# Attention, Fourier mixing and feed-forward on one core: packed constants, cross-wise folds, special columns as two column groups, a new order

## The chip, the cores and the metric

The kernel runs on one core of one Trainium2 chip. A time is the device time of one execution in microseconds (us); what is compared is the median over several executions. A profile is one execution recorded by the hardware: its span runs from the first to the last instruction, and the time of that execution is a little longer than its span.

The engines are TensorE (PE, whose weight loads are listed as PEld), VectorE (DVE), ScalarE (ACT), GpSimd (POOL) and SyncE (SP, which only issues DMAs here). Each works through its own instructions in program order and waits on semaphores for the others.

## The reference

Three stages follow each other for 8 batches, 576 positions and 8 heads of 64 (512 columns).

```python
# attention: local band plus a pooled copy (positions averaged by 4)
q_d, k_d, v_d = (t.reshape(B, H, S // 4, 4, D).mean(3) for t in (q, k, v))
out_up = np.repeat(softmax_attention(q_d, k_d, v_d), 4, axis=2)
out_local = softmax_attention(q, k, v, mask=abs(i - j) < 4)
x = (out_up + out_local) -> [8, 576, 512]
# mixing
mixed = real(fft(fft(x, axis=1), axis=2))
u = x + mixed
# feed-forward, 512 -> 2048 -> 512
un = (u - mean(u)) / sqrt(var(u) + 1e-6)
out = u + relu(un @ w_ch1) @ w_ch2
```

## The kernel before

**Attention.** A `Unit` is a span of 128 positions of one batch (5 per batch, 40 in all). Its steps are `load` (queries and keys, 512 KB), `load_v`, `sum_in` (sums over 4 positions, DVE, line 697), `scores` (PE: four matmuls that put the band mask into the banks, line 707, and then 16 of queries with keys, line 714), `maxima` (DVE, line 726), `exps` (ACT), `transpose_p` (PE, with the identity as an operand, line 746), `copy_p`, `values` and `result`, which leaves the rows of the front half of a batch in `xa` and those of the back half, mirrored, in `xb`. `Pooled` does the same for the averaged sequence of a batch, once all five `sum_in` are done; its first PE step is line 567, and it leaves its rows in `odt`.

**Mixing.** The transform of a real sequence is done by folding. `Mix.half_sum` (DVE, line 838) and `half_difference` (POOL, line 841) make `xa + xb` and `xa - xb`. `channels` (DVE, line 849) adds to, or takes from, each its own mirror over the columns, `fold` (DVE and POOL, line 862) halves the columns once more, `sequence` (PE, line 887) multiplies by cosines and sines over positions, and `mix` (PE) by those over columns. Columns 0 and 256 have no mirror: `split_z` copies them to `zs`, `sequence_z` (PE, line 902) takes 4 matmuls with 66 columns of weights each, which add up in one bank, and `z_high` and `z_low` store the 4 rows of the result in two parts in `yz`, which `clear_yz` has set to zero.

**Feed-forward.** Rows are taken in nine blocks of 512. `Quarter` decodes the weights, which are given as 64-bit floats: `fetch` (SP), `size` (ACT), `clamp` (POOL), `join` (three DVE instructions, lines 448, 451 and 454), `high` (ACT) and `low` (POOL), 64 times. `Block.first` (line 1266) and `Block.second` (lines 1286 to 1288) are the two products, and `Block.finish` (DVE, line 1292) empties a bank of the second into the output rows. Blocks 0 and 1 start with the first five of 16 weight chunks and go on when more are decoded; blocks 3 and up use a scheme with fewer products (line 1204).

**Order.** Each call of `at` takes its place from the table `TURNS`, one row of numbers for each step; all steps are issued in the order of these places, on every engine, and PSUM banks are handed out in that order. Steps from block 3 on have times worked out by formula in place of table entries.

**Start.** SP issues the identity `ident` first, then the loads. POOL issues two DMAs that convert to 16 bits on the way, `identb` (line 480) and `maskb` (line 482); both are operands of the band mask's matmuls. Meanwhile PE runs 40 matmuls of 128 columns on zeros (`WARM_UP`, line 1400).

Of the kernel before, what the change touches and what calls it, by code (L numbers as in the profile page):

```python
# [22 lines left out]
ZCOLS = 66  # L23
# [4 lines left out]
        55, 125, 253, 392, 518, 667, 797, 918,  # L28
    ),
    "Pooled.copy_v": (  # L30
        59, 129, 262, 399, 521, 670, 806, 926,
    ),
    "Pooled.scores": (
        41, 22, 34, 150, 78, 115, 263, 204, 230, 411, 346, 361, 523, 483, 501, 671, 627, 646, 803, 755, 764,
        934, 866, 899,
    ),
    "Pooled.maxima": (
        43, 26, 39, 152, 85, 118, 271, 212, 232, 417, 352, 379, 529, 490, 516, 680, 632, 647, 820, 757, 770,
        940, 873, 904,
    ),  # L40
    "Pooled.exps": (
        54, 32, 40, 165, 101, 121, 272, 220, 248, 424, 353, 384, 533, 498, 520, 686, 634, 665, 821, 762, 782,
        944, 875, 919,
    ),
    "Pooled.transpose_p": (
        65, 38, 42, 188, 104, 136, 303, 233, 268, 436, 369, 414, 557, 509, 526, 711, 644, 682, 840, 767, 810,
        951, 881, 931,
    ),
    "Pooled.copy_p": (
        70, 47, 64, 200, 120, 148, 308, 240, 270, 437, 382, 423, 563, 519, 541, 712, 662, 687, 847, 775, 818,  # L50
        953, 886, 941,
    ),
    "Pooled.values": (
        72, 62, 66, 211, 145, 151, 316, 275, 285, 446, 403, 432, 576, 527, 551, 720, 675, 717, 856, 809, 845,
        967, 927, 947,
    ),
    "Pooled.result": (
        79, 63, 71, 217, 147, 161, 322, 277, 297, 456, 405, 448, 580, 536, 556, 721, 679, 719, 869, 811, 857,
        970, 935, 956,
    ),  # L60
    "Pooled.store": (
        109, 187, 404, 453, 653, 768, 868, 973,
    ),
    "Pooled.pack": (
        95, 229, 332, 489, 606, 734, 891, 976,
    ),
    "Mix.half_sum": (
        108, 134, 127, 258, 237, 254, 360, 395, 373, 515, 506, 517, 642, 639, 643, 751, 788, 774, 907, 913,
        932, 993, 980, 996,
    ),  # L70
    "Mix.half_difference": (
        111, 97, 113, 241, 216, 225, 356, 368, 370, 508, 485, 547, 626, 684, 683, 793, 829, 795, 900, 905,
        912, 1005, 978, 994,
    ),
    "Mix.channels": (
# [4 lines left out]
    ),  # L80
    "Mix.fold": (
# [4 lines left out]
    ),  # L86
    "Mix.split_z": (
        133, 157, 189, 267, 380, 421, 468, 558, 637, 700, 787, 815, 922, 939, 1002, 1006,
    ),
    "Mix.sequence_z": (  # L90
        185, 290, 458, 559, 714, 824, 986, 1015,
    ),
    "Mix.z_high": (
        207, 304, 469, 573, 715, 835, 991, 1053,
    ),
    "Mix.z_low": (
        214, 311, 486, 578, 725, 843, 1013, 1083,
    ),
    "Mix.sequence": (
        202, 191, 169, 170, 323, 337, 336, 330, 487, 479, 452, 450, 619, 610, 585, 590, 752, 743, 735, 727,  # L100
        848, 854, 878, 887, 1001, 997, 1000, 990, 1040, 1059, 1071, 1076,
    ),
    "Mix.sequence_out": (
        206, 180, 350, 342, 495, 462, 624, 591, 760, 758, 860, 892, 1012, 1017, 1073, 1105,
    ),
    "Mix.mix": (
        231, 246, 228, 239, 354, 374, 378, 398, 355, 408, 497, 512, 507, 582, 631, 655, 641, 673, 678, 696,
        778, 781, 765, 769, 911, 979, 921, 954, 903, 897, 1085, 1093, 1034, 1084, 1112, 1219, 1203, 1291,
        1143, 1152,
    ),  # L110
# [4 lines left out]
    "Mix.unfold": (
        255, 257, 243, 251, 385, 381, 400, 416, 442, 427, 524, 538, 604, 594, 664, 661, 676, 692, 708, 707,
        807, 805, 779, 791, 1044, 1045, 1033, 1007, 920, 917, 1145, 1134, 1096, 1110, 1250, 1259, 1297, 1303,
        1177, 1184,
    ),
    "Mix.store_mixed": (  # L120
        298, 438, 616, 716, 901, 1064, 1238, 1307,
    ),
    "Mix.store_local": (
        112, 117, 287, 261, 389, 406, 534, 542, 691, 702, 756, 837, 906, 957, 989, 998,
    ),
    "Mix.store_ends": (
        543, 858, 1042, 1286,
    ),
    "Unit.load": (
        0, 4, 13, 1, 8, 50, 52, 14, 35, 48, 76, 182, 141, 91, 143, 252, 307, 222, 329, 249, 375, 434, 209,  # L130
        413, 415, 513, 588, 548, 572, 540, 697, 600, 672, 690, 654, 789, 784, 825, 763, 801,
    ),
    "Unit.sum_in": (
        3, 9, 16, 6, 12, 58, 68, 51, 44, 57, 168, 192, 197, 183, 198, 341, 345, 328, 339, 276, 463, 476, 473,
        477, 449, 611, 605, 613, 599, 587, 747, 674, 693, 713, 738, 808, 846, 862, 827, 859,
    ),
# [12 lines left out]
    "Unit.exps": (
        11, 15, 36, 73, 56, 89, 114, 124, 155, 173, 226, 238, 282, 260, 325, 288, 394, 409, 454, 467, 504,  # L150
        562, 570, 584, 586, 615, 629, 677, 706, 744, 740, 802, 814, 832, 852, 896, 908, 960, 950, 972,
    ),
    "Unit.transpose_p": (
        19, 25, 53, 77, 90, 99, 132, 159, 160, 205, 250, 245, 305, 289, 331, 410, 401, 422, 455, 472, 528,
        568, 583, 593, 607, 622, 636, 699, 718, 745, 772, 816, 828, 870, 867, 910, 930, 964, 958, 982,
    ),
    "Unit.copy_p": (
        21, 29, 69, 80, 102, 106, 137, 172, 171, 213, 269, 256, 317, 300, 338, 419, 418, 426, 465, 474, 554,
        575, 595, 602, 617, 649, 638, 709, 728, 753, 785, 836, 851, 871, 880, 914, 936, 969, 968, 983,
    ),  # L160
    "Unit.values": (
        28, 67, 86, 87, 107, 164, 146, 190, 178, 218, 295, 306, 321, 333, 348, 431, 420, 464, 471, 496, 560,
        603, 612, 620, 633, 736, 701, 726, 766, 759, 823, 853, 872, 885, 888, 938, 955, 981, 971, 987,
    ),
# [3 lines left out]
    ),  # L168
    "constants": (
        135,  # L170
    ),
    "clear_yz": (
        176,
    ),
# [1372 lines left out]
```

## Time and profile before

| | |
|---|---|
| median of 3 runs | 1107.03 us (1103.9 to 1108.41) |
| time of the profiled execution | 1109.62 us |
| its span | 1107.6 us |
| busy in the span: PE, DVE, ACT, POOL | 1064.3, 635.5, 401.4, 349.3 us |
| mean granted clock of PE | 0.994 |
| HBM read and written | 166.86 MB, 45.42 MB |

The busy time of an engine is an average over stages with different limits, so the rows below are by stage. A busy PE is one with a matmul in flight; how many matmuls share the array can't be seen from it, only from the distances between starts. In a row of a timeline a group's length is that of its last end, and the next group may start before it.

### The profile page before, as it was taken

What the parts mean: (1) busy time and instruction counts of PE and PEld (TensorE: products, weight loads), DVE (VectorE), ACT (ScalarE), POOL (GpSimd) and SP (SyncE); (2) the same over time, 40 slices, a digit from 0 to 9 for tenths busy, and PEclk for the clock granted to TensorE, in tenths of its full rate; (3) what the DMA queues carried; (4) which work ended last, traced back from release to release, by engine and by line L of the source; (5) the groups of instructions that cost most, each with busy time, mean ns of one, the idle gap of its engine ahead of it and who ended that gap; (6) DMA issues with size and microseconds to landing.
All of it is one profiled execution on the core that took longest, in us unless ns stands there. A gap on an engine that the chain in (4) does not pass through costs nothing.

```text
span 1107.6 us, 24297 instructions
## 1 busy us (share of the span) xinstructions
PE 1064.3 (96%) x9316; PEld 892.8 (81%) x9316; DVE 635.5 (57%) x1298; ACT 401.4 (36%) x1122; POOL 349.3 (32%) x501
## 2 busy tenths in 40 slices
PE   6899999999989999999999999999999999999998
PEld 5676676777768788888788898899988889988997
DVE  5888989898797884442423533534443443353333
ACT  5765676655434442221312321231231232232121
POOL 1323223234554545655612131140230331221000
PEclk8999999999999999999999999999999999999999
DMA  7767668763845555748619546955954964975641
GB/s 269 227 199 236 198 227 250 226 182 115 228 99 170 156 156 185 168 140 223 185 65 283 192 155 197 300 160 176 318 177 141 294 210 150 243 252 180 218 153 38
DMA packets 121451, 214.36 MB, mean 194 GB/s; under 512 B 14576, under 2 KB 30992, under 8 KB 121208
## 3 DMA queue, kind: packets, MB, share of 16 engines
q1 hardware_dynamic: 110056, 191.97, 52.7%
q0 software_dynamic: 11280, 20.84, 10.6%
q8 instruction: 74, 1.21, 0.4%
q14 instruction: 41, 0.34, 0.1%
HBM read 166.86 MB, written 45.42 MB: 192 GB/s over the span
## 4 chain that ended last, share of the span: by engine, by line
PE 71%; DMA 12%; DVE 9%; issue 3%; ACT 2%; SPq 1%; POOL 1%; DVEq 0%; ACTq 0%; POOLq 0%
PE banks L1204 19%; PE banks L1286 10%; PE banks L1287 10%; PE banks L1288 10%; PE banks L1266 8%; PE banks L887 3%; DMA w1l<-ut 3%; DMA qkT<-in_qk_dram 3%; DMA raw<-in_wq_dram 2%; PE banks L926 2%; PE banks L616 1%; DMA w1h<-ut 1%; PE banks L1133 1%; PE banks L774 1%; PE banks L746 1%
## 5 line engine op out<-in xcount | busy, mean ns | idle before, releaser
L1286 PE MATMUL banks<-w2h,hh 128*128 128x512 f32 x576 | 228.0, 396 | 0.0
L1287 PE MATMUL banks<-w2l,hh 128*128 128x512 f32 x576 | 225.4, 391 | 0.0
L1288 PE MATMUL banks<-w2h,hl 128*128 128x512 f32 x576 | 224.9, 390 | 0.2 <-DVE hl L1274 0.2
L1270 ACT ACTIVATE hh<-row 128x512 fp32r<-128x512 f32 x96 | 60.6, 632 | 282.9 <-DVE row L1229 188.2
L1229 DVE TENSOR_TENSOR row<-wt,banks 128x256 f32<-128x256 f32 x192 | 80.3, 418 | 141.9 <-PE banks L1204 137.5
L1274 DVE SCALAR_TENSOR_TENSOR hl<-row,hh 128x512 fp32r<-128x512 f32 x96 | 68.9, 718 | 119.6 <-ACT hh L1270 119.6
L1288 PEld LDWEIGHTS banks<-w2h,hl 128*128 128x128 f32 x576 | 108.2, 188 | 24.3 <-DVE hl L1274 0.6
L1286 PEld LDWEIGHTS banks<-w2h,hh 128*128 128x128 f32 x576 | 108.5, 188 | 19.8
L1287 PEld LDWEIGHTS banks<-w2l,hh 128*128 128x128 f32 x576 | 108.6, 188 | 19.3
L1266 PE MATMUL banks<-unT,w1h 128*128 128x512 f32 x384 | 103.7, 395 | 3.5 <-DVE ut L1292 2.2
L1266 PEld LDWEIGHTS banks<-unT,w1h 128*128 128x128 f32 x384 | 72.4, 189 | 20.1 <-DVE ut L1292 2.7
L1103 POOL DMA_DIRECT2D ut<-ux x40 | 34.8, 941 | 162.4 <-DMA ut<-um 133.1
L1274 DVE SCALAR_TENSOR_TENSOR hl<-banks,hh 128x512 fp32r<-128x512 f32 x48 | 32.6, 686 | 74.6 <-ACT hh L1270 74.5
L1224 ACT COPY wt<-banks 128x256 f32<-128x256 f32 x96 | 35.7, 372 | 97.2 <-PE banks L1204 97.0
L733 ACT ACTIVATE sb<-banks,mx 128x64 f32<-128x64 f32 x320 | 69.8, 329 | 1.4 <-PE banks L746 0.2
L887 PE MATMUL banks<-seq,f 128*128 128x290 f32 x256 | 67.8, 414 | 0.9 <-issue 0.6
L1204 PE MATMUL banks<-w1h,w1h 128*128 128x256 f32 x384 | 62.0, 283 | 2.6 <-DMA w1h<-ut 1.5
L1204 PE MATMUL banks<-w1h,w1l 128*128 128x256 f32 x384 | 62.5, 285 | 2.0 <-DMA w1l<-ut 1.5
L1270 ACT ACTIVATE hh<-banks 128x512 fp32r<-128x512 f32 x48 | 28.5, 597 | 98.5 <-PE banks L1287 62.4
L1204 PE MATMUL banks<-unT,w1h 128*128 128x256 f32 x432 | 63.3, 283 | 0.7 <-DVE row L1229 0.7
L1204 PEld LDWEIGHTS banks<-unT,w1h 128*128 128x128 f32 x432 | 59.8, 191 | 4.7 <-DVE row L1229 0.9
L1204 PE MATMUL banks<-unT,w1l 128*128 128x256 f32 x432 | 63.2, 282 | 0.0
(122 smaller groups left out, 1944.0 us busy)
## 6 DMA issues: line engine op xcount, KB each, us to landing
w1l<-ut SPq DMA_DIRECT2D x96, 256.0 KB
w1h<-ut SPq DMA_DIRECT2D x96, 256.0 KB
qkT<-in_qk_dram SPq DMA_DIRECT2D x40, 512.0 KB
w1h<-ub SPq DMA_DIRECT2D x72, 256.0 KB
w1l<-ub SPq DMA_DIRECT2D x72, 256.0 KB
raw<-in_wq_dram SPq DMA_DIRECT2D x64, 256.0 KB
vaug<-in_vw_dram SPq DMA_DIRECT2D x40, 260.0 KB
out_dram<-ut SPq DMA_DIRECT2D x36, 256.0 KB
```

Of the source, the lines that this page charges most:

```text
L733: nc.scalar.activation(out=self.sb[:, hp, z], in_=self.sc[:, z, hp], func=AF.Exp, scale=0.125, bias=self.mx[:, z, hp : hp + 1],)
L887: nc.tensor.matmul(y, l, r, start=(i == 0), stop=(i == len(mms) - 1))
L1103: nc.gpsimd.dma_start(out=to, in_=ux[b][k0 : k0 + m, :], accum_op=ALU.add)
L1204: nc.tensor.matmul(into, w[:, y, c, :], both[z][:, c, :], start=(start and i == 0), stop=(i == len(mms) - 1), skip_group_check=True)
L1224: nc.scalar.copy(out=joins[k].bitcast(F32), in_=self.ps[x])
L1229: nc.vector.tensor_add(out=place(to), in0=place(a), in1=self.ps[x])
L1266: nc.tensor.matmul(hps, a[:, c, :], unT[:, x, c, :], start=(i == 0), stop=(i == len(mms) - 1))
L1270: nc.scalar.activation(out=hh, in_=self.hps[f], func=AF.Relu)
L1274: nc.vector.scalar_tensor_tensor(out=hl, in0=self.hps[f], scalar=0.0, in1=self.hh[f].bitcast(F32), op0=ALU.max, op1=ALU.subtract)
L1286: nc.tensor.matmul(acc, hh, w2h, start=start, stop=False)
L1287: nc.tensor.matmul(acc, hh, w2l, start=False, stop=False)
L1288: nc.tensor.matmul(acc, hl, w2h, start=False, stop=stop)
```

## The change

**Constants at the start.** Identity and mask arrive as 16-bit numbers that the host has packed in pairs into 32-bit words, in one tile `bits` (48 KB), by SP's first DMA. The full identity moves from SP's queue to POOL's, as the first DMA there. `WARM_UP` goes from 40 to 28.

**Cross-wise folds.** `half_sum` and `half_difference` become `cross`: `p` is `xa` plus the column mirror of `xb` (DVE), `q` is `xb` plus the column mirror of `xa` (POOL), 255 columns each where the former two took 512. `channels` then takes `p + q` and `p - q`, so each of its instructions reads what both engines made.

**Special columns.** `zs` has 32 columns a slot where it had 66. Of the four matmuls of `sequence_z` two write rows 0 to 31 and two write rows 32 to 63 of the bank. `z_high` and `z_low` store all 64 rows of each part, so `clear_yz` goes, and `signs` sums the two groups in `mix`. `split_z` adds the columns from `xa` and `xb` on POOL, where ACT had copied them.

**Order.** Every entry of `TURNS` is new up to the start of the fourth block.

```diff
-WARM_UP = 40
+WARM_UP = 28
...
-    nc.sync.dma_start(out=ident, in_=c_ident)
+    nc.gpsimd.dma_start(out=ident, in_=c_ident)
...
-    identb = pd.tile([P, P], BF16, name="identb", bufs=1)
-    nc.gpsimd.dma_start(out=identb, in_=c_ident)
-    maskb = pd.tile([P, W], BF16, name="maskb", bufs=1)
-    nc.gpsimd.dma_start(out=maskb, in_=c_mask)
+    bits = pd.tile([P, P + W], BF16, name="bits", bufs=1)
+    nc.sync.dma_start(out=bits.bitcast(F32), in_=c_bits)
+    identb, maskb = bits[:, :P], bits[:, P:]
...
-        def half_sum(self, t):
-            nc.vector.tensor_add(out=halves[0][:, t, :DM], in0=xa[:, t], in1=xb[:, t])
-
-        def half_difference(self, t):
-            nc.gpsimd.tensor_sub(out=halves[1][:, t, :DM], in0=xa[:, t], in1=xb[:, t])
+        def cross(self, t, back):
+            near, far = (xb, xa) if back else (xa, xb)
+            (nc.gpsimd if back else nc.vector).tensor_tensor(
+                out=crossed[back][:, t, 1:HD], in0=near[:, t, 1:HD], in1=far[:, t, DM - 1 : HD : -1], op=ALU.add
+            )
...
-            src = odt[:, 0] if t == NSL else halves[odd][:, t]
+            if t == NSL:
+                a, b = odt[:, 0, 1:HD], odt[:, 0, DM - 1 : HD : -1]
+            else:
+                a, b = (x[:, t, 1:HD] for x in crossed)
...
-            nc.scalar.copy(out=z[:, :, 0:2], in_=x)
+                nc.scalar.copy(out=zs[:, NSL:, 0:2], in_=odt[:, 0:1, cols])
             else:
+                nc.gpsimd.tensor_add(out=zs[:, :NSL, 0:2], in0=xa[:, :, cols], in1=xb[:, :, cols])
...
-            y = self.yzp = bank(self, "yz", ZCOLS)[:, 0, :KEPT]
-            mms = self.slots(zs, 0)
-            for i, (l, r) in enumerate(mms):
-                nc.tensor.matmul(y, l, r, start=(i == 0), stop=(i == len(mms) - 1))
+            y = self.yzp = bank(self, "yz", 2 * ZCOLS)[:, 0, :KEPT]
+            for i, (l, r) in enumerate(self.slots(zs, 0)):
+                g = i % 2 * ZCOLS
+                nc.tensor.matmul(y[g : g + ZCOLS], l, r, start=(i < 2), stop=(i >= 2), skip_group_check=True)
```

The order shows at three places. On DVE, the first sums (697 before, 690 after the change), maxima (726, 719) and pooled maxima (572, 565) at the program's start, before:

```order
L697 TENSOR_REDUCE sums<-qkT 128x8x32
L726 TENSOR_REDUCE mx<-banks 128x8
L697 TENSOR_REDUCE sums<-qkT 128x8x32 x2
L726 TENSOR_REDUCE mx<-banks 128x8
L697 TENSOR_REDUCE sums<-qkT 128x8x32
L697 TENSOR_REDUCE sums<-qkT 128x8x15
L697 TENSOR_REDUCE sums<-qkT 128x8x17
L726 TENSOR_REDUCE mx<-banks 128x8
L572 TENSOR_REDUCE mxd<-banks 128x4
```

and of the change:

```order
L690 TENSOR_REDUCE sums<-qkT 128x8x32
L719 TENSOR_REDUCE mx<-banks 128x8
L690 TENSOR_REDUCE sums<-qkT 128x8x32
L719 TENSOR_REDUCE mx<-banks 128x8
L690 TENSOR_REDUCE sums<-qkT 128x8x32
L719 TENSOR_REDUCE mx<-banks 128x8
L690 TENSOR_REDUCE sums<-qkT 128x8x15
L690 TENSOR_REDUCE sums<-qkT 128x8x17
L719 TENSOR_REDUCE mx<-banks 128x8
L690 TENSOR_REDUCE sums<-qkT 128x8x32
L565 TENSOR_REDUCE mxd<-banks 128x4
```

Sums and maxima now take turns, and four units have their maxima ahead of the fifth unit's sum, where two had.

On PE, around the second batch's `sequence_z`, before:

```order
L714 MATMUL banks<-qkT 64x64 x16
L616 MATMUL banks<-vsum,ptd 64x65 x16
L746 MATMUL banks<-ident,sb 128x128 x4
L902 MATMUL banks<-seq,z 66x290 x4
L774 MATMUL banks<-vaug,pT 64x65 x16
```

and of the change:

```order
L700 MATMUL banks<-bits 64x256
L707 MATMUL banks<-qkT 64x64 x16
L891 MATMUL banks<-seq,z 32x290 x4
L609 MATMUL banks<-vsum,ptd 64x65 x16
L767 MATMUL banks<-vaug,pT 64x65 x16
```

The four matmuls, now of 32 columns of weights, stand between the scores of a unit and the pooled values, where a transpose had stood ahead of them.

On DVE, where block 1's first five weight chunks are done and its banks are emptied (line 1292 before, 1282 after the change) between joins of decoded weights (448, 451 and 454; 442, 445 and 448), before:

```order
L1292 TENSOR_TENSOR ut_4797<-banks,ut_4797 128x512
L1292 TENSOR_TENSOR ut_4798<-banks,ut_4798 128x512
L448 TENSOR_SCALAR wt<-wt 128x256
L451 SCALAR_TENSOR_TENSOR wt<-raw,wt 128x256
L454 SCALAR_TENSOR_TENSOR wt<-raw,wt 128x256
L448 TENSOR_SCALAR wt<-wt 128x256
L451 SCALAR_TENSOR_TENSOR wt<-raw,wt 128x256
L454 SCALAR_TENSOR_TENSOR wt<-raw,wt 128x256
L1292 TENSOR_TENSOR ut_4800<-banks,ut_4800 128x512
```

and of the change:

```order
L1282 TENSOR_TENSOR ut_4785<-banks,ut_4785 128x512
L442 TENSOR_SCALAR wt<-wt 128x256
L445 SCALAR_TENSOR_TENSOR wt<-raw,wt 128x256
L448 SCALAR_TENSOR_TENSOR wt<-raw,wt 128x256
L1282 TENSOR_TENSOR ut_4787<-banks,ut_4787 128x512
L1282 TENSOR_TENSOR ut_4788<-banks,ut_4788 128x512
```

Three banks are emptied with one join between them, where two joins stood ahead of the third.

## Rows read from the trace of the kernel before

**Rows 1.** Busy time by stage: us, PE, PEld, DVE, ACT, POOL, clock, DMA, GB/s.
```profile
0.00:20.00 20.00, 12.49 (x240) 10.76 (x240) 9.53 (x15) 7.74 (x28) 3.65 (x15) 0.83 0.92 342
20.00:60.00 40.00, 33.01 (x783) 23.93 (x787) 35.22 (x76) 30.99 (x115) 9.52 (x15) 0.96 0.63 210
60.00:280.00 220.00, 211.25 (x3779) 155.54 (x3770) 197.94 (x421) 138.99 (x486) 71.07 (x97) 1.00 0.66 203
280.00:400.00 120.00, 113.73 (x496) 90.66 (x495) 99.78 (x199) 49.42 (x121) 64.97 (x105) 0.99 0.56 160
400.00:1108.00 708.00, 693.78 (x4037) 611.89 (x4035) 293.00 (x590) 174.30 (x375) 200.08 (x270) 1.00 0.63 191
```

**Rows 2.** PE timeline, 0 to 14 us: start, length, work, idle before and releaser.
```profile
1.01 4.45 PE L1400 MATMUL banks<-raw 128*128 128x128 bf16 x40 [1.01 <-DVE raw L1397]
8.54 0.30 PE L707 MATMUL banks<-maskb,identb 64*64 64x256 bf16 x4 [3.08 <-DMA maskb<-in_c_mask_dram]
8.65 0.90 PE L714 MATMUL banks<-qkT 64*64 64x64 f32 x32
```

**Rows 3.** DVE timeline, 0 to 15 us.
```profile
5.00 1.22 DVE L697 TENSOR_REDUCE sums<-qkT 128x256 f32<-128x1024 f32 x1 [4.04 <-DMA qkT<-in_qk_dram]
9.64 0.69 DVE L726 TENSOR_REDUCE mx<-banks 128x8 f32<-128x512 f32 x1 [3.43 <-PE banks L714]
10.25 2.33 DVE L697 TENSOR_REDUCE sums<-qkT 128x256 f32<-128x1024 f32 x2
```

**Rows 4.** PE timeline, 12.5 to 16.5 us.
```profile
15.55 1.23 PE L567 MATMUL banks<-sums 64*64 64x160 f32 x16 [2.45 <-DVE sums L697]
```

**Rows 5.** DMA issues: last figure is median us from issue to landing.
```profile
identb<-in_c_ident_dram POOLq DMA_DIRECT2D x1, 32.0 KB, 5.1
```

**Rows 6.** POOL timeline, 0 to 4 us.
```profile
1.25 0.74 POOL L480 DMA_DIRECT2D identb<-in_c_ident_dram  x1 [0.82 <-POOLq L1530]
```

**Rows 7.** PE timeline, 85.9 to 89 us.
```profile
86.27 2.12 PE L902 MATMUL banks<-seq,z 128*66 128x290 f32 x8
88.32 0.70 PE L774 MATMUL banks<-vaug,pT 64*64 64x65 f32 x32
```

**Rows 8.** PE timeline, 181.9 to 184.2 us.
```profile
182.35 1.69 PE L541 MATMUL banks<-vaug,poolm 128*32 128x260 f32 x20
183.97 0.50 PE L567 MATMUL banks<-sums 64*32 64x160 f32 x16
```

**Rows 9.** DVE groups by shape, 0 to 290 us: busy us, mean ns.
```profile
L838 DVE TENSOR_TENSOR xs<-xa,xb 128x512 f32<-128x512 f32 x24 | 19.1, 800 | 0.3 <-DVE f L862 0.3
...
L849 DVE TENSOR_TENSOR w<-xm 128x255 f32<-128x255 f32 x24 | 12.8, 542 | 0.1
...
L849 DVE TENSOR_TENSOR w<-xs 128x255 f32<-128x255 f32 x24 | 10.5, 437 | 0.0
```

**Rows 10.** POOL groups by shape, 0 to 300 us.
```profile
L841 POOL TENSOR_TENSOR xm<-xa,xb 128x512 f32<-128x512 f32 x24 | 32.5, 1368 | 34.4 <-DVE xb L794 21.1 <-DMA xa<-rest 6.6 <-DVE rs L791 5.2
L862 POOL TENSOR_TENSOR f<-w 128x256 f32<-128x256 f32 x32 | 26.7, 839 | 43.7 <-DVE w L849 30.5 <-DVE rs L791 12.8 <-DVE rsd L628 0.4
```

**Rows 11.** PE timeline, 365 to 380 us.
```profile
365.83 1.07 PE L1266 MATMUL banks<-unT,w1h 128*128 128x512 f32 x4
...
368.55 0.39 PE L1286 MATMUL banks<-w2h,hh 128*128 128x512 f32 x1
...
373.67 1.71 PE L1266 MATMUL banks<-unT,w1h 128*128 128x512 f32 x4 [2.24 <-DVE ut L1292]
...
378.12 0.40 PE L1286 MATMUL banks<-w2h,hh 128*128 128x512 f32 x1
```

**Rows 12.** DVE timeline, 362 to 378 us.
```profile
367.79 1.28 DVE L1292 TENSOR_TENSOR ut<-banks,ut 128x512 f32<-128x512 f32 x2
...
371.81 0.28 DVE L448 TENSOR_SCALAR wt<-wt 128x256 int32<-128x256 int32 x1
...
372.93 0.68 DVE L1292 TENSOR_TENSOR ut<-banks,ut 128x512 f32<-128x512 f32 x1
```

More of the change, by code (lines that the diff above doesn't have):

```diff
@@ L22 @@
 TAIL = KEPT - 256
-ZCOLS = 66
+ZCOLS = 32
 ITEM = 1.6
@@ L60 @@
+        973, 929, 957,
     ),
     "Pooled.store": (
-        109, 187, 404, 453, 653, 768, 868, 973,
+        105, 245, 360, 542, 675, 808, 865, 970,
     ),
     "Pooled.pack": (
-        95, 229, 332, 489, 606, 734, 891, 976,
+        109, 208, 350, 494, 614, 748, 903, 989,
     ),
[L67 to L73, printed above, removed]
+    "Mix.cross": (
[3 rows of a table added]
@@ L117 @@
[L117 to L118 removed]
+        320, 318, 238, 239, 402, 401, 397, 400, 458, 449, 523, 520, 556, 560, 685, 668, 650, 659, 690, 691,
+        841, 858, 835, 836, 902, 910, 1016, 988, 947, 951, 1113, 1107, 1071, 1103, 1195, 1171, 1274, 1300,
+        1269, 1251,
     ),
     "Mix.store_mixed": (
[L121 removed]
+        359, 465, 635, 715, 880, 1048, 1153, 1301,
@@ L168 @@
     ),
     "constants": (
[L170 to L173, printed above, removed]
+        80,
     ),
     "close_b": (
-        1008,
+        994,
     ),
     "close_a": (
-        1014,
+        1015,
     ),
     "close_e": (
-        1119,
+        1088,
     ),
     "close_d": (
-        1317,
+        1319,
     ),
     "Block.load": (
[3 rows of a table removed]
[3 rows of a table added]
     ),
     "Block.stats": (
-        995, 877, 909, 890, 1131, 1163, 1192, 1158, 1655, 1620, 1649, 1610, 1806, 1823, 1814, 1837,
+        932, 990, 859, 784, 1121, 1137, 1130, 1148, 1628, 1626, 1668, 1652, 1774, 1780, 1792, 1821,
@@ L229 @@
-        1888, 1892, 1895,
+        1240, 1241, 1243, 1233, 1357, 1404, 1360, 1363, 1565, 1568, 1569, 1582, 1714, 1691, 1696, 1702, 1885,
+        1890, 1888, 1883,
     ),
     "Block.store": (
-        1612, 1599, 1575, 1574, 1750, 1714, 1724, 1757, 1889, 1891, 1894, 1896,
+        1590, 1587, 1580, 1594, 1720, 1693, 1727, 1724, 1895, 1896, 1894, 1892,
     ),
     "Block.turn_copy": (
-        1838, 1846, 1836, 1844,
+        1851, 1848, 1846, 1854,
     ),
     "Block.add_up": (
-        1841, 1848,
+        1853, 1858,
@@ L346 @@
     c_ident: bass.AP,
-    c_mask: bass.AP,
+    c_bits: bass.AP,
     c_seq: bass.AP,
@@ L813 @@
     zs = psq.tile([P, NSL + 1, ZCOLS], F32, name="z")
-    halves = [pf.tile([P, NSL, DM + 2], F32, name=f"x{h}") for h in "sm"]
-    for t in (zs, *(t[:, :, DM:] for t in halves)):
-        nc.gpsimd.memset(t, 0.0)
+    crossed = [pf.tile([P, NSL, HD], F32, name=f"x{h}") for h in "pq"]
+    nc.gpsimd.memset(zs, 0.0)
     def constants():
@@ L822, in constants @@
         nc.gpsimd.dma_start(out=signs, in_=c_signs)
-    def clear_yz():
-        nc.scalar.mul(out=yz, in_=seqm[:, 0, 0:2, :].rearrange("p a k -> p (a k)"), mul=0.0)
     class Mix:
@@ L847, in channels @@
                 self.w[t] = psq.tile([P, 2, HD], F32, name="w", bufs=2)
-            src = odt[:, 0] if t == NSL else halves[odd][:, t]
+            if t == NSL:
+                a, b = odt[:, 0, 1:HD], odt[:, 0, DM - 1 : HD : -1]
+            else:
+                a, b = (x[:, t, 1:HD] for x in crossed)
             nc.vector.tensor_tensor(
-                out=self.w[t][:, odd, 1:HD],
-                in0=src[:, 1:HD],
-                in1=src[:, DM - 1 : HD : -1],
-                op=ALU.subtract if odd else ALU.add,
+                out=self.w[t][:, odd, 1:HD], in0=a, in1=b, op=ALU.subtract if odd else ALU.add
             )
@@ L982, in plan @@
             for slot in reversed(range(NSL)):
-                at(self.half_sum, slot)
-                at(self.half_difference, slot)
+                for back in range(2):
+                    at(self.cross, slot, back)
             for slot in reversed(range(NSL + 1)):
@@ L1414, in _constants @@
     j = np.arange(64)
-    mask = np.where(np.abs(i[:, None] - j[None, :]) < 4, 0.0, -8e9).astype(np.float32)
+    mask = np.where(np.abs(i[:, None] - j[None, :]) < 4, 0.0, -8e9)
+    pairs = (np.concatenate([ident, mask], axis=1).astype(np.float32).view(np.uint32) >> 16).reshape(P, -1, 2)
+    bits = (pairs[:, :, 0] | pairs[:, :, 1] << 16).astype(np.uint32).view(np.float32)
     k1 = np.arange(KEPT)
@@ L1462, in _constants @@
                     pool[(w ^ n) * W + i, n, u * P // 4 + groups_of(u).index(g)] = 1.0
-    out = {"c_ident": ident, "c_mask": mask, "c_seq": seq, "c_chan": chan, "c_signs": signs, "c_pool": pool}
+    out = {"c_ident": ident, "c_bits": bits, "c_seq": seq, "c_chan": chan, "c_signs": signs, "c_pool": pool}
     out = {n: np.ascontiguousarray(a, dtype=np.float32) for n, a in out.items()}
```

140 lines of the change are left out of this document (68 added, 72 removed), and 105 rows, old and new, of the table TURNS.

## The prediction

> **What bounds the kernel now.** I read the busy time by stage first, then the timelines of PE and DVE in the stage where PE is idle most.
>
> The table by stage [rows 1] is to be read down the PE column. From 60 to 280 us PE is busy for 211.25 of 220 us, from 400 to the end for 693.78 of 708: there PE sets the pace, and only fewer or better shared matmuls shorten it. The first 60 us are different: PE is busy for 12.49 + 33.01 = 45.5 of 60 us. From 280 to 400 us it is busy for 113.73 of 120. Of 1108 us PE is idle for about 44, and 14.5 of them lie in the first 60.
>
> The next engine is DVE: 35.22 of 40 us from 20 to 60 and 197.94 of 220 from 60 to 280, that is 88 to 90%. It follows PE closely, so work taken from PE alone pays only while DVE keeps up.
>
> At the start the chain is plain. PE ends its 40 warm-up matmuls at 5.46 us and stands idle for 3.08 us until the mask has landed; the first scores start at 8.65 [rows 2]. DVE has had the first unit's queries and keys at 5.00, has summed them by 6.22, and then waits 3.43 us for those scores [rows 3]. PE later waits 2.45 us for DVE's sums [rows 4]: DVE is late by what it lost.
>
> **The change part by part.**
>
> *Constants first.* The packed constants are SP's first DMA, with 48 KB where the identity had 64, so the loads behind them start as before and the first unit is there at 5.0 us, as DVE's row shows [rows 3]. The warm-up is over by then (28 of 40 matmuls in 4.45 us are 3.1, so at 4.1 us) [rows 2]. Scores can start at 5.0 and last 1.0 (8.65 to 9.64), so DVE goes from its first sum straight to the maxima at 6.2 where it came to them at 9.64: the 3.43 us of waiting are gone. Does something else come late next? Loads of 512 KB at the 342 GB/s of that stage take 1.5 us each [rows 1], an estimate for all traffic going to them; DVE needs 1.22 + 0.69 = 1.9 us a unit [rows 3] in the alternating order, so loads stay ahead. Five sums of 1.22 (the one in two parts taken as one) and 4 maxima of 0.69 end at 5.0 + 6.1 + 2.8 = 13.9 us, and the first pooled scores can then run, against 15.55 [rows 4], with two more maxima done, worth 1.4. That is 3 us, the 3.4 again within what the order changes. The identity comes by POOL's queue: issued at 1.25 us [rows 6] and 5.1 us to landing for half its size [rows 5], about 6.4 us. Its first user is a transpose after maxima and exponentials, at about 9, so its move is free; without that margin of 2.6 us each us of lateness would be one of PE's.
>
> **Term 1: 3.4 us.** Bounds: nothing, if PE's later waits for DVE and ACT in the first 60 us take it up, and 6 us, if the alternating order also removes the 2.45 us wait.
>
> *Special columns.* Before, 4 matmuls are 8 records, from 86.27 us to the next group's start at 88.32: 2.05 us, 0.256 each, one after the other [rows 7]. Do two groups of 32 columns run side by side? The row that answers is that of the pooled sums of values, with all 128 rows as well: 20 records of 260 columns, 16 of them on 32 columns of weights and 4 on 64, in 1.62 us (182.35 to 183.97) [rows 8]. At 0.256 x 260/290 = 0.23 each, one after the other would take 4.6 us. Four at a time for the 16 and two at a time for the 4 are 6 rounds, 1.38 us. So they do share the array, and going from one shape to another costs the rest, 0.24 us for two shapes, 0.12 each. For the changed group: 4 rounds of 0.256 and 0.12 make 1.15 us, 0.90 less; eight batches give 7.2 us. All eight stand in the stretch where PE is busy for 96%, so I count them in full.
>
> **Term 2: 7.2 us.** Bounds: 0, if the two groups do not overlap, and 8 x 1.02 = 8.2 with no cost for the shape.
>
> The Trainium skill speaks against part of this: TensorEngine Tiling, section Tiling Modes, says that a change of the tiling mode, unlike one of the tile, drains the engine. The 66 columns of before ran without column groups, the 32 need them, so by that rule there is a drain on the way in and one on the way out. By rows 8 a shape costs 0.12 us, which agrees with a drain that is short; if each of 16 drains took a round of 0.256, the term would be 8 x (1.02 - 0.51) = 4.1 us.
>
> *Folds.* The half sum takes DVE 800 ns for 24 instructions; its successor has the shape of `channels`, 437 to 542 [rows 9], so I take 0.49 and DVE saves 24 x 0.31 = 7.4 us (6.2 to 8.7). POOL goes from 1368 ns to about the 839 of its fold over 256 columns [rows 10]: 24 x 0.53 = 12.7 us less, and eight additions of two columns back, at most 0.84 each. ACT loses eight small copies and one clearing. All of this I cost at nothing for the time: PE's 96% covers it. If it were uncovered it would be worth up to DVE's 7.4 us. What it does is keep DVE at its share: 197.9 - 7 of 220 - 7 is again 90%, so DVE does not take over when PE gets shorter. The new wait, of `channels` for both engines, is for POOL's 0.84 us against the 1.37 that the odd half waited for before; behind it on DVE stand folds and maxima, for which PE waits. I take it as 0, from -0.5 to +0.5 us a batch.
>
> *Order.* Where the first five chunks of block 1 end, PE waits 2.24 us for DVE to empty a bank, and the next 12 products take 4.45 us (373.67 to 378.12) where the same 12 took 2.72 (365.83 to 368.55) [rows 11]: that is a PE at half its clock, 1.2 for 2.4 GHz, after an idle stretch. The stall costs 2.24 + 1.73 = 4.0 us. On DVE a join (0.28, 0.42 and 0.42 us at 371.81 to 372.59) is directly ahead of the bank's emptying at 372.93 [rows 12]. In the new order one join stands between three emptyings where two stood ahead of the third, which by these rows is 1.1 us earlier; but PE comes to this place about 10 us earlier too, and the weights are decoded by ACT, POOL, DVE and DMA at a pace that the change does not touch. I take 0, from a gain of 4.0 to a loss of 4.0.
>
> **Sum.** 3.4 + 7.2 = 10.6 us. The profiled execution took 1109.6 us (span 1107.6 and 2.0 around it), which gives 1099.0; it lies 2.6 above the median shown, against which the sum is 1096.4. I predict 1097. About 0.5%, 5.5 us, is what a measurement of this kernel can tell from no change.
>
> **The rivals.**
>
> *The two groups run one after the other, or drains eat the gain.* For it: the two matmuls of a group add into one bank and must wait for each other, and neighbours in the new order are of other shapes. Against it: rows 8, with the same width of weights. Only term 1 is left: about 1103.5. Chance 0.08.
>
> *The gain is given back at the hand-over.* Between 280 and 400 us DVE is busy for 99.8 of 120 us and decoding feeds PE. If decoding cannot come earlier, PE reaches the products 10 us sooner and waits there, once more at half clock. For it: the stall of rows 11 is of this kind. Against it: DVE too is free earlier, by 3.4 + 7. Two more stalls of 4.0 would make 1105; I give 1102 to 1107 a chance of 0.13.
>
> *Slower: a load comes late in the new order.* SP issues in order, and a load that stands behind a store that waits for results lands late by that wait. If this hits a unit, DVE's sums, then scores and PE stand for the wait; DVE's first load took 4.04 us of waiting [rows 3]. It decides from four such waits on, each with a stretch at half clock (4.04 + 1.73 = 5.8 us): 1097 + 23 = 1120. With three, it is about 1114. For it: all places are new. Against it: PE's idle time from 60 to 280 us is 8.75 us in all [rows 1], so the present order has hardly any. Chance 0.08.
>
> **How the numbers follow.** The forecast (both terms, the hand-over about as before) has 0.71, with its own range from 1090 to 1102. The range for 8 in 10 runs from 1088 (term 1 at 6, term 2 at 8.2 and the stall of 4.0 gone, 18 us in all) to 1107, which takes in both rivals that end near the time before. Faster by over 0.5%, below 1101.5: the forecast and a little of the hand-over, 0.73. Within it: the rest of those two rivals, 0.19. Slower: 0.08.
>
> **What would show it.** Scores start at about 5 us and DVE has no wait of 3 us before its first maxima. A group of special columns lasts 1.1 to 1.3 us to the next start, in 4 rounds. PE's busy time falls by some 7 us, the whole of it before 290 us; idle time before 60 us falls by 3 or more. DVE's cross takes 0.45 to 0.55 us. If block 0's first product comes 10 us earlier but the end does not, the hand-over has it. If special columns still take 2 us a batch, the first rival holds. More than 20 us of PE idle from 60 to 280 us would make the last one true.

## The result, and the profile after the change

The changed kernel takes 1093.53 us (median of 4 runs, 1093.14 to 1095.61) against 1107.49 us of the kernel before on the same chip: ratio 0.9884, 95% interval 0.9858 to 0.9909, faster by about 13 us. Taken a second time beside other kernels it had 0.984 [0.9804, 0.9875]. Both ratios are used below: what a version loses or gains against the changed kernel is given as the two differences, each of which has an interval of about 3 to 5 us to either side.

The profile shows an execution of 1093.14 us with a span of 1091.2, which is 16.4 less than before. The first lines of the page (busy time and share of each engine):

```profile
span 1091.2 us, 24252 instructions
PE 1052.7 (96%) x9304; PEld 887.5 (81%) x9304; DVE 620.4 (57%) x1298; ACT 398.2 (36%) x1113; POOL 333.2 (31%) x506
```

Busy time by stage, columns as in [rows 1]:

```profile
0.00:20.00 20.00, 15.95 (x254) 11.99 (x254) 12.30 (x16) 12.87 (x49) 2.81 (x11) 1.00 0.90 350
20.00:60.00 40.00, 36.03 (x879) 27.57 (x879) 37.13 (x86) 29.17 (x107) 9.36 (x20) 1.00 0.66 228
60.00:280.00 220.00, 206.88 (x3711) 155.87 (x3700) 194.10 (x430) 139.36 (x476) 67.84 (x114) 0.99 0.69 210
```

In the first 60 us PE is busy for 52.0 us where it was 45.5 [rows 1]. From 60 to 280 us it is busy for 4.4 us less, so it is idle for 13.1 of 220 us, not 8.75 (10.5 in the second profile of the changed kernel). That is the first sign against the prediction: in the stretch where PE was to set the pace it now waits more.

The first product of the feed-forward part, before and after, and PE's busy time up to it:

```profile
292.60 1.20 PE L1266 MATMUL banks<-unT,w1h 128*128 128x512 f32 x4 [0.96 <-ACT unT L1139]
281.18 1.20 PE L1256 MATMUL banks<-unT,w1h 128*128 128x512 f32 x4 [1.91 <-DVE unT L1132]
```

```profile
0.00:292.60 292.60, 268.39 (x4841) 199.43 (x4841) 253.90 (x535) 184.37 (x642) 92.87 (x140) 0.98 0.68 215
0.00:281.20 281.20, 258.89 (x4830) 195.45 (x4830) 244.73 (x532) 182.06 (x632) 80.40 (x146) 0.99 0.70 222
```

It comes 11.4 us earlier, with 9.5 us less of PE's work ahead of it; the other 5.0 of the span's 16.4 us are won behind it.

The timeline of PE at the start answers to [rows 2] and [rows 4]:

```profile
1.01 3.17 PE L1389 MATMUL banks<-raw 128*128 128x128 bf16 x28 [1.01 <-DVE raw L1386]
4.11 0.43 PE L700 MATMUL banks<-bits 64*64 64x256 bf16 x4
5.15 1.13 PE L707 MATMUL banks<-qkT 64*64 64x64 f32 x32 [0.62 <-DMA qkT<-in_qk_dram]
...
13.81 2.41 PE L560 MATMUL banks<-sums 64*64 64x160 f32 x32 [0.98 <-DVE sums L690]
```

And DVE's, for [rows 3]:

```profile
5.13 1.22 DVE L690 TENSOR_REDUCE sums<-qkT 128x256 f32<-128x1024 f32 x1 [4.18 <-DMA qkT<-in_qk_dram]
6.38 0.69 DVE L719 TENSOR_REDUCE mx<-banks 128x8 f32<-128x512 f32 x1
6.98 1.21 DVE L690 TENSOR_REDUCE sums<-qkT 128x256 f32<-128x1024 f32 x1
```

Scores start at 5.15 us instead of 8.65, DVE goes from its first sum to the first maxima without a wait, and the pooled scores start at 13.81 instead of 15.55, as the prediction had them (13.9).

PE's timeline at a group of special columns, for [rows 7]:

```profile
112.52 1.17 PE L891 MATMUL banks<-seq,z 128*32 128x290 f32 x8 [0.24 <-DVE xa L787]
113.62 0.69 PE L767 MATMUL banks<-vaug,pT 64*64 64x65 f32 x32
```

The next group starts 1.10 us after it, where it was 2.05: 0.95 saved, 0.90 forecast. So the two column groups do run beside each other. By the prediction's 0.256 a record, 8 records in pairs are 1.02 us, so what lies on top is 0.08 us. The Trainium skill states that a change of the tiling mode drains the engine (TensorEngine Tiling (Array Packing), section Tiling Modes). A drain, if there is one here, is shorter than a round of 0.256. It isn't priced by itself: before, too, a group of 64*64 stood behind the special columns [rows 7], and what the 2.05 us hold of such a change is in the 0.256.

The folds on DVE by shape, 0 to 290 us (busy us, mean ns), for [rows 9]:

```profile
L841 DVE TENSOR_TENSOR w<-xp,xq 128x255 f32<-128x255 f32 x48 | 19.1, 426 | 1.3 <-POOL f L851 1.2
L828 DVE TENSOR_TENSOR xp<-xa,xb 128x255 f32<-128x255 f32 x24 | 13.7, 578 | 3.6 <-DMA xa<-rest 3.6
```

`cross` takes 578 ns on DVE, longer than the 490 taken but less than the 800 of the half sum. The stall at the hand-over [rows 11] is gone. Where DVE empties block 1's second and third bank, PE goes on, and the products that follow keep their short time (2.72 us from 363.88 to 366.60, as at 365.83 in [rows 11]):

```profile
359.93 1.28 DVE L1282 TENSOR_TENSOR ut<-banks,ut 128x512 f32<-128x512 f32 x2
363.88 1.07 PE L1256 MATMUL banks<-unT,w1h 128*128 128x512 f32 x4
366.60 0.39 PE L1276 MATMUL banks<-w2h,hh 128*128 128x512 f32 x1
```

### The profile page after: what moved, and what is told of

The parts are those of the page before. It is cut to its first block, busy times and chain, and to the rows that moved or that the text cites. A ratio compares the mean times of both kernels' runs of the same rounds, so it can differ in the third digit from the quotient of the medians.

```text
span 1091.2 us, 24252 instructions
## 1 busy us (share of the span) xinstructions
PE 1052.7 (96%) x9304; PEld 887.5 (81%) x9304; DVE 620.4 (57%) x1298; ACT 398.2 (36%) x1113; POOL 333.2 (31%) x506
## 3 DMA queue, kind: packets, MB, share of 16 engines
q0 software_dynamic: 11024, 20.86, 10.6%
## 4 chain that ended last, share of the span: by engine, by line
PE 72%; DMA 12%; DVE 10%; issue 3%; ACT 2%; SPq 1%; POOL 1%; DVEq 0%; ACTq 0%; POOLq 0%
PE banks L1194 18%; PE banks L1276 11%; PE banks L1277 11%; PE banks L1278 11%; PE banks L1256 10%; PE banks L876 3%; DMA w1l<-ut 2%; DMA xa<-rest 1%; PE banks L916 1%; PE banks L1123 1%; DMA w1l<-ub 1%; DMA raw<-in_wq_dram 1%; DMA w1h<-ut 1%; DMA qkT<-in_qk_dram 1%; PE banks L767 1%
```

## The experiments

After the result there were several candidates for what gives the 13 us, and the expectations name them. Theory A, in the first four, is the prediction's view (PE sets the pace and covers the folds), with what is left of the gain put down to the order. Theory L, set up after the first eight runs: in the new order the stretch from 60 to 280 us is paced by loads and stores and by the waits around them, so that PE work there costs little; in the old order PE sets the pace. Rival N: the part pays nowhere. Theory D: DVE sets the pace, so that what the folds take from DVE is what counts. Rival P: POOL's half of the folds does. Rival C: what the start saves is given back before the feed-forward part. Each of the three groups below has its own runs of the kernel before beside it (medians 1109.5, 1111.38 and 1111.65 us).

### One part undone at a time

**Constants undone.** The changed kernel with the mask and the identity loaded as before, and 40 warm-up matmuls:

```diff
-    bits = pd.tile([P, P + W], BF16, name="bits", bufs=1)
-    nc.sync.dma_start(out=bits.bitcast(F32), in_=c_bits)
-    identb, maskb = bits[:, :P], bits[:, P:]
+    identb = pd.tile([P, P], BF16, name="identb", bufs=1)
+    nc.gpsimd.dma_start(out=identb, in_=c_ident)
+    maskb = pd.tile([P, W], BF16, name="maskb", bufs=1)
+    nc.gpsimd.dma_start(out=maskb, in_=c_mask)
```

> The changed kernel with its constants as before: the identity first on SP, identity and mask for the band converted by two DMAs of POOL, 40 warm-up matmuls. Theory A (the constants are worth the 3.43 us that DVE waited, the rest of the gain at the start is the new order's): about 1097 us, first scores at 8.6, and what PE has done by 60 us is about 3.4 us less than in the changed kernel. Rival B (the early start is worth all of the 8 us that PE is ahead by 60 us): about 1101. Rival C (later waits take it up): 1093 to 1094.

Measured: 1094.67 us, 0.986 [0.9842, 0.9877], between the changed kernel's two ratios: no loss that can be measured, though against the lower ratio one of 3 us would still fit. The wait itself is back, as its DVE timeline shows:

```profile
10.17 0.69 DVE L720 TENSOR_REDUCE mx<-banks 128x8 f32<-128x512 f32 x1 [3.16 <-PE banks L708]
```

So in the new order a wait of 3.2 us at the start is not seen at the end. Single profiles can't settle it: the changed kernel's own two have spans of 1091.2 and 1088.7 us.

**Special columns undone.** The changed kernel with one group of 66 columns again, and the clearing that it needs:

```diff
-ZCOLS = 32
+ZCOLS = 66
...
-            for i, (l, r) in enumerate(self.slots(zs, 0)):
-                g = i % 2 * ZCOLS
-                nc.tensor.matmul(y[g : g + ZCOLS], l, r, start=(i < 2), stop=(i >= 2), skip_group_check=True)
+            mms = self.slots(zs, 0)
+            for i, (l, r) in enumerate(mms):
+                nc.tensor.matmul(y, l, r, start=(i == 0), stop=(i == len(mms) - 1))
```

> The changed kernel with the special columns as before: 66 columns of weights, four matmuls one after the other, two parts of 4 rows, clearing of yz. Theory A (PE sets the pace where they stand, so 0.9 to 0.95 us a batch is worth all of itself): 1100.5 to 1101.5 us, 2.05 us from the first record to the next group. Rival (DVE sets the pace there): under 1097.

Measured: 1096.14 us, 0.9875 [0.9851, 0.9899], 1 us better and 4 us worse than the changed kernel by its two ratios: no loss that can be measured, and by both together hardly one of 7 us. Its page's lines of span and engines:

```profile
span 1088.4 us, 24251 instructions
PE 1056.6 (97%) x9304; PEld 890.1 (82%) x9304; DVE 622.2 (57%) x1298; ACT 398.4 (37%) x1114; POOL 332.1 (31%) x506
```

and those of the changed kernel's second profile:

```profile
span 1088.7 us, 24252 instructions
PE 1047.3 (96%) x9304; PEld 882.8 (81%) x9304; DVE 619.1 (57%) x1298; ACT 398.4 (37%) x1113; POOL 333.6 (31%) x506
```

PE does 9.3 us more work in the same span and is idle for 31.8 us instead of 41.4; 5.7 of the 9.3 lie between 20 and 280 us, where all eight groups stand. In this pair, each the fastest execution of its kernel, what the two groups save PE spends waiting.

**Folds undone.** Half sum and half difference at the places of `cross`, the special columns copied by ACT from the half sum, which in four of the eight batches puts that step just behind the half sum:

```diff
-        def cross(self, t, back):
-            near, far = (xb, xa) if back else (xa, xb)
-            (nc.gpsimd if back else nc.vector).tensor_tensor(
-                out=crossed[back][:, t, 1:HD], in0=near[:, t, 1:HD], in1=far[:, t, DM - 1 : HD : -1], op=ALU.add
-            )
+        def half_sum(self, t):
+            nc.vector.tensor_add(out=halves[0][:, t, :DM], in0=xa[:, t], in1=xb[:, t])
+
+        def half_difference(self, t):
+            nc.gpsimd.tensor_sub(out=halves[1][:, t, :DM], in0=xa[:, t], in1=xb[:, t])
...
-                nc.gpsimd.tensor_add(out=zs[:, :NSL, 0:2], in0=xa[:, :, cols], in1=xb[:, :, cols])
+                z, x = zs[:, :NSL], halves[0][:, :, 0 : HD + 1 : HD]
+            nc.scalar.copy(out=z[:, :, 0:2], in_=x)
```

> The changed kernel with the half sum over 512 columns on DVE and the half difference on POOL, and the special columns copied by ACT from the half sum. Theory A (hidden behind PE): 1093 to 1095 us, with DVE some 7 us busier. Rival (DVE sets the pace in part of the first 290 us): 1097 to 1101.

Measured: 1105.81 us, 0.9965 [0.995, 0.998], 9 to 14 us worse than the changed kernel. ACT's timeline shows where it starts, and two later waits of the same copy:

```profile
44.70 0.20 ACT L663 COPY z<-xs 128x6 f32<-128x6 f32 x1 [5.39 <-DVE xs L626]
...
45.04 1.74 ACT L524 ACTIVATE sb<-banks,mx 128x64 f32<-128x64 f32 x8
...
144.16 0.20 ACT L663 COPY z<-xs 128x6 f32<-128x6 f32 x1 [4.30 <-DVE xs L626]
...
272.46 0.20 ACT L663 COPY z<-xs 128x6 f32<-128x6 f32 x1 [10.58 <-DVE xs L626]
```

and PE's what follows:

```profile
46.22 1.12 PE L537 MATMUL banks<-ident,sb 128*128 128x128 f32 x4 [4.05 <-ACT sb L524]
```

A copy of 0.20 us waits 5.39 us at the head of ACT's queue for the half sum; the exponentials stand behind it, and PE waits 4.05 us for them. In the changed kernel POOL makes these columns from `xa` and `xb`. At this place the execution falls behind the changed kernel's by 4.0 us (DVE's next `rsd` ends at 50.51 for 46.20, after it had been 0.3 us behind), of 10.1 at its end. The price of the old folds is so at least in part this copy's place, and not DVE's time; the run doesn't part the two.

**Order undone.** The changed code with every place of before; `cross` stands where the half sum and half difference stood, 6 of its 48 steps a little earlier, as `channels` now needs both. The first line of one table:

```diff
     "Unit.load": (
-        2, 0, 7, 17, 6, 21, 40, 56, 36, 71, 107, 120, 128, 133, 130, 139, 234, 225, 236, 285, 308, 389, 446,
+        0, 4, 13, 1, 8, 50, 52, 14, 35, 48, 76, 182, 141, 91, 143, 252, 307, 222, 329, 249, 375, 434, 209,
```

> The changed kernel's code in the order of places of before; the two cross-wise sums take the places of half sum and half difference. Theory A (order adds the rest of the gain, some 3 to 4 us, at the start and at the hand-over): 1096 to 1098 us, with the start at 5 us and the short special columns kept. Rival (the parts alone make the whole gain): 1093 to 1095. Rival (the new parts need the new order): 1100 and more.

Measured: 1105.73 us, 0.9955 [0.9936, 0.9975], 8 to 13 us worse. PE's timeline and DVE's at the largest stall before 60 us:

```profile
52.45 0.43 PE L497 MATMUL banks<-bits 64*64 64x256 bf16 x4 [2.20 <-DVE xa L584]
```

```profile
51.70 0.69 DVE L584 TENSOR_TENSOR xa<-banks,rs 128x512 f32<-128x512 f32 x1 [5.06 <-DMA ux<-xa]
```

DVE may not write `xa` until a store has read it; it stands for 5.06 us, and PE for 2.20 behind it. The store is not late in SP's queue: it was issued earlier than in the kernel before. But POOL issued the loads of the cosines and sines (1160 and 512 KB) right behind its start, here:

```profile
40.35 2.31 SPq L765 DMA_DIRECT2D ux<-xa  x4
40.66 0.58 POOL L609 DMA_DIRECT2D seq<-in_c_seq_dram  x1
```

and in the kernel before, where DVE has no such wait:

```profile
42.13 2.44 SPq L978 DMA_DIRECT2D ux<-xa  x4
44.40 0.59 POOL L820 DMA_DIRECT2D seq<-in_c_seq_dram  x1
```

From the store's last issue to DVE's write are 9.0 us here (42.71 to 51.70), 6.7 in the kernel before (44.61 to 51.28, without a wait) and 5.5 in the version with the constants alone, below (42.27 to 47.72, without a wait, the loads 3.1 us behind the store's start). POOL comes to these loads 3.7 us sooner than in the kernel before, after shorter sums (0.72 to 1.01 us for 1.28). DVE too comes to its write sooner. In DVE's order this execution leads the kernel before by 4.6 us ahead of the wait (`odt` at 45.91 for 50.51) and is 0.4 behind after it (`mxd` at 52.31 for 51.88), so it loses 5.0 us here; at the end it leads by 5.6. The new order has these loads at 23.05 us, far ahead of the stores. That the loads hold the store up is read from these traces; no run moved them alone.

### Is it DVE's or POOL's time?

**The changed kernel once more**, as the measure for the next three:

> The changed kernel itself, beside the three that follow. Ratio to before 0.986 to 0.991.

Measured: 1095.42 us, 0.984 [0.9804, 0.9875].

**More work for DVE.** Behind each `cross` of DVE an addition of 160 columns, its result unused:

```diff
+            if not back:
+                nc.vector.tensor_tensor(out=more, in0=near[:, t, 0:160], in1=far[:, t, 0:160], op=ALU.add)
```

> The changed kernel with one more DVE addition of 160 columns after each cross-wise sum on DVE, 24 in all of about 0.32 us (7.7 us of DVE, what the folds save there), its result unused. Theory D (DVE, not PE, sets the pace in the first 290 us; this is why the folds were worth 9 us and the shorter special columns nothing): 5 to 9 us over the run of the changed kernel. Rival P (the folds help by what they take from POOL): under 3 us over it. The prediction's view (PE covers DVE): 0 to 1.

Measured: 1093.72 us, 0.9849 [0.981, 0.9888]. The group of its DVE work shows that it was done:

```profile
L833 DVE TENSOR_TENSOR more<-xa,xb 128x160 f32<-128x160 f32 x24 | 10.9, 453 | 0.0
```

DVE does 10.9 us more, which is more than the folds were to save (7.4), and no loss is seen. The runs spread from 1092.8 to 1103.7 us, so a loss of up to 5 would be hidden; Theory D's 5 to 9 is unlikely, and DVE's time is not what the undone folds cost.

**More work for POOL.** The same for POOL's half:

```diff
+            if back:
+                nc.gpsimd.tensor_tensor(out=more, in0=near[:, t, 0:160], in1=far[:, t, 0:160], op=ALU.add)
```

> The changed kernel with one more POOL addition of 160 columns after each cross-wise sum on POOL, 24 in all of about 0.5 us (12 us of POOL, what the folds save there), its result unused. Theory D: under 3 us over the changed kernel, as POOL has room. Rival P: 5 to 9 us over it, by the wait of channels for POOL's sum.

Measured: 1096.44 us, 0.984 [0.9805, 0.9875], with 24 additions of 638 ns, 15.3 us. The same holds for Rival P's 5 to 9.

**Work moved from DVE to POOL**, the adding folds of two of the four slots:

```diff
-            eng, op = (nc.gpsimd, ALU.subtract) if minus else (nc.vector, ALU.add)
+            eng, op = (nc.gpsimd if minus or t in (3, 1) else nc.vector), (ALU.subtract if minus else ALU.add)
```

> The changed kernel with the adding fold of two of the four slots moved from DVE to POOL, 16 of about 0.45 us: 7 us less on DVE, 13 us more on POOL. Theory D: 2 to 7 us under the changed kernel, less what later folds on POOL hold PE up. Prediction's view: 0, or slower by POOL's longer folds.

Measured: 1094.6 us, 0.9844 [0.9804, 0.9884]: no gain that can be seen.

### One part alone in the old kernel, and the loads taken away

**Special columns alone.** The kernel before with the two groups, everything else as it was (the edit of the second experiment, the other way round):

```diff
-ZCOLS = 66
+ZCOLS = 32
```

> The kernel before with the special columns alone changed (32 columns of weights in two groups, 64 rows stored, no clearing of yz); folds, constants and order are those of before. Theory L (the old order is paced by PE, the new one from 60 to 280 us by DMA landings that DVE and PE wait for, so that PE's shorter work pays only in the old): 5 to 8 us under before. Rival N (the shorter special columns pay nowhere): within 2 us of before.

Measured: 1112.33 us, 0.9991 [0.9974, 1.0009]: nothing, or at most 3 us. This is Term 2 by itself, in the order in which it was worked out, and theory L's half on the old order falls with it. Its page:

```profile
span 1112.0 us, 24296 instructions
PE 1060.4 (95%) x9316; PEld 888.1 (80%) x9316; DVE 632.6 (57%) x1298; ACT 400.4 (36%) x1121; POOL 349.8 (31%) x501
```

Before, PE was idle for 43.3 us of its span; here for 51.6. The place where the saved time goes can be seen, in the kernel before on PE and DVE:

```profile
166.24 2.12 PE L887 MATMUL banks<-seq,f 128*128 128x290 f32 x8
169.92 0.70 PE L774 MATMUL banks<-vaug,pT 64*64 64x65 f32 x32 [1.56 <-DVE xa L794]
```

```profile
164.95 1.22 DVE L697 TENSOR_REDUCE sums<-qkT 128x256 f32<-128x1024 f32 x1 [2.64 <-DMA qkT<-in_qk_dram]
```

and at the same place in this kernel, with a later one of PE:

```profile
162.73 2.12 PE L884 MATMUL banks<-seq,f 128*128 128x290 f32 x8
168.83 1.15 PE L774 MATMUL banks<-vaug,pT 64*64 64x65 f32 x32 [3.98 <-DVE xa L794]
...
251.47 1.68 PE L541 MATMUL banks<-vaug,poolm 128*32 128x260 f32 x16 [2.60 <-DMA vaug<-in_vw_dram]
```

```profile
163.85 1.22 DVE L697 TENSOR_REDUCE sums<-qkT 128x256 f32<-128x1024 f32 x1 [5.04 <-DMA qkT<-in_qk_dram]
```

PE comes to this place 3.5 us earlier (162.73 for 166.24). The queries and keys that DVE needs land only 1.1 us earlier (163.85 for 164.95), so DVE waits 5.04 us instead of 2.64 and PE 3.98 instead of 1.56: 2.4 us are given back at one landing. By its place in the order that load is the first of these two, before and here:

```profile
156.75 0.89 SPq L681 DMA_DIRECT2D qkT<-in_qk_dram  x2
154.38 0.90 SPq L681 DMA_DIRECT2D qkT<-in_qk_dram  x2
```

SP issued it 2.4 us earlier, and it took 9.5 us until DVE could use it instead of 8.2: the place in SP's queue took 1.1 of the 3.5 us and the transfer 1.3. After its longer wait PE works at half clock (granted 0.50 from 168.1 to 174.9 us, 1.00 in the kernel before), and its next eight matmuls on `seq` take nearly twice as long, before and here:

```profile
171.59 2.22 PE L887 MATMUL banks<-seq,f 128*128 128x290 f32 x8
171.01 4.12 PE L884 MATMUL banks<-seq,f 128*128 128x290 f32 x8
```

PE begins them 0.6 us ahead of the kernel before and begins what follows 1.3 us behind it (175.06 for 173.74). So the lead of 3.5 us is gone, by the landing and by the clock. At 251.47 PE waits 2.60 us more, for a load of values, where the kernel before has no such wait. The first product of the feed-forward part starts at 295.0 us, in the kernel before at 292.6. These are one execution each, of 1114.05 and 1109.62 us, from different sets of runs; what the runs as a whole say is the ratio.

**Constants alone**, the first experiment the other way round:

```diff
-WARM_UP = 40
+WARM_UP = 28
```

> The kernel before with the constants alone changed (packed constants first on SP, identity on POOL's queue, 28 warm-up matmuls). Theory L: the 3.4 us stay, since the old order is paced by PE: 3 to 4 us under before. Rival N (what is won at the start is lost in the waits that follow): within 2 us of before.

Measured: 1105.95 us, 0.9946 [0.9925, 0.9967], 6.0 us faster than before (3.7 to 8.3). PE's timeline at its start:

```profile
5.46 0.69 PE L713 MATMUL banks<-qkT 64*64 64x64 f32 x32 [1.13 <-DMA qkT<-in_qk_dram]
5.97 0.29 PE L706 MATMUL banks<-bits 64*64 64x256 bf16 x4
8.70 1.13 PE L713 MATMUL banks<-qkT 64*64 64x64 f32 x32 [2.43 <-DMA qkT<-in_qk_dram]
...
13.37 1.07 PE L566 MATMUL banks<-sums 64*64 64x160 f32 x12
```

PE now waits for the second unit's load (2.43 us), but the pooled scores start at 13.37, without the wait of 2.45 us of [rows 4]; the first product starts at 287.3 us, 5.3 earlier than before. Both expectations, 3 to 4 us and under 2, were too low.

**Without loads.** The changed kernel loads no queries, keys and values from the eleventh unit on, and computes these units from those of earlier ones:

```diff
+            if self.u >= 10:
+                self.qkT = units[self.u - 5].qkT
+                return
...
+            if self.u >= 10:
+                self.va = units[self.u - 5].va
+                return
```

> The changed kernel without the loads of queries, keys and values from the eleventh unit on; these units read what units 6 to 10 loaded, so 30 units of the attention are computed from the wrong data, with the same work on the engines. Theory L: DVE's waits for loads (4.7 us from 60 to 280 us) and PE's for values (2.5) go, 3 to 7 us under the changed kernel. Rival (loads pace nothing): within 2 us of it.

Measured: 1082.16 us, 0.9725 [0.9708, 0.9742], 13 to 18 us faster than the changed kernel. From 60 to 280 us, columns as in [rows 1]:

```profile
60.00:280.00 220.00, 216.76 (x3775) 165.65 (x3776) 200.98 (x453) 144.61 (x489) 75.88 (x125) 1.00 0.48 131
```

PE is idle for 3.2 us there, not 13.1, with all the other edits in place: with these loads gone it hardly waits.

**The same with the special columns of before** (again `ZCOLS` 66):

```diff
-ZCOLS = 32
+ZCOLS = 66
```

> The same without those loads, but with the special columns as before (66 columns of weights, one after the other). Theory L: with the loads out of the way PE paces the stage, so this is 5 to 8 us slower than the kernel without loads beside it. Rival N: within 2 us of it.

Measured: 1086.37 us, 0.9763 [0.9743, 0.9782]: 4.2 us slower than the last, with no overlap of their runs. Only here, with the loads gone, is Term 2 seen at the end, and then with 4.2 of its 7.2 us, between what Theory L and Rival N expected.

## Why the prediction was right in the sum and wrong in its terms

**The total** of 1097 us, with a gain of 10.6, was near the 13 measured. That is luck: the first term is larger than forecast, the second is not seen at the end, and the two that were put at nothing make up the rest. The signs named beforehand could not tell: scores at 5.15 us, 6.5 us less idle time before 60 us, 1.10 us a group and 9.5 us less work of PE before the first product came true or nearly, and only `cross` (578 ns for 450 to 550) did not.

**Term 1, the start** (3.4 us, bounds 0 to 6). The mechanism was right, row by row. Alone it measures 6.0 us [3.7, 8.3], which fits the upper bound: the order of before loses both waits, that for the mask and that for the sums, the second without the alternating order to which the prediction tied it. In the new order its undoing costs nothing that can be measured, so it isn't shown to add to the rest.

**Term 2, the special columns** (7.2 us). Right on PE (0.95 us a group for 0.90) and wrong at the end: 0.9991 in the old order, and nothing that can be measured in the new. The step that failed is "All eight stand in the stretch where PE is busy for 96%, so I count them in full", and before it "there PE sets the pace" for 60 to 280 us. PE was busy for 96% and still met landings that hardly moved when it came earlier; in the profiled execution its saved time turned into the longer wait at 168.83 us, the half clock behind it, and a new wait at 251.47. The bound of 0 was in the prediction, but for the case that the groups don't overlap, which is not what happened.

**Folds at nothing, order at nothing.** The gain over the constants alone came from here. In the old order, constants, folds and special columns together (0.9955) are no better than the constants alone (0.9946). The new places then bring 8 to 13 us. With the old folds they don't (0.9965), in a version where the waiting copy of ACT has a part in it. So in the old order no part but the constants was seen to pay, and the rest of the gain came only with new order and new code together. The prediction costed the order at the start and at the hand-over, where it gave 0 with up to 4.0 of gain: that stall is gone, and in the profiled executions 5.0 us are won behind the first product. What it had no row for are the DMAs and copies before 60 us: a store behind POOL's large loads (5.06 us of DVE's time, 5.0 lost) and ACT's copy (5.39, 4.0 lost). That PE's 96% covers the folds was no reason, though added work of DVE and POOL shows no loss either: these runs point to what its place holds up, not to the amount of work.

**The rivals.** The groups overlap, so the first didn't come. The second was right that a gain can be given back, and wrong in where: not at the hand-over, where the stall is gone, but at landings before it. The third, a load that comes late in the new order, didn't come as a loss; a load that doesn't come earlier when PE does is what absorbs Term 2 in the old order, in part by its place in SP's queue.

**What stays open.** That loads as a whole limit the stretch is shown by their removal. It also takes away DMA traffic (131 GB/s for 210), and whether the wait of SP in front of a load or the transfer itself sets the landing was told apart at one place only, where both had a share. Nor was it tried what the new order alone, without any of the other parts, would do, or the old folds with the special columns still made by POOL, or the old order with the large loads early. Part of the gain may be clock: the mean granted clock of the changed kernel's runs is 0.996 and 0.995, of the three sets of the kernel before 0.993, 0.991 and 0.993, and with the folds undone 0.991. One minus the clock, times the run's time, is 5 us for the changed kernel and 8 to 10 before, an upper bound of what the lower clock cost; fewer stalls would explain it, but that wasn't tested. Differences below about 0.3 to 0.5% are not resolved by these runs.

## What to carry to other kernels

An engine that is busy for 96% need not set the pace: before its saved time is counted, look at the few waits that are left in the stretch, and ask whether what ends each of them (a landing, a store that frees a buffer) would come earlier too; if not, the saving ends at the first of them. An order by hand and the code that it orders are best tried together, and the smallest instruction at the head of an engine's queue, or a large load issued beside a store, can carry the price. A sum that comes out right does not show that its terms are: each part alone, and each part undone, tells it.

## What the runs showed of the hardware

A saving on PE cost clock as well: after the wait of 3.98 us, where it had been 1.56, the granted clock was 0.50 for 6.8 us, the same 32 matmuls took 1.15 us instead of 0.70 and the next 8 on `seq` 4.12 instead of 2.22, so that a lead of 3.5 us ended as a lag of 1.3: a saving that ends in one longer wait can give back more than itself. With 1.67 MB of loads issued 0.3 us behind a store's start, DVE could write the store's source 9.0 us after its last issue; with the loads 2.3 and 3.1 us behind, it wrote without a wait after 6.7 and 5.5. Two groups of 32 columns with 128 rows ran beside each other, 8 records in 1.10 us to the next start, which is 0.08 us over four rounds of 0.256.
